# A ConvNeXt-V2 block on one core: from fourteen slots between a block's convolution and its expansion to twelve

## Chip, cores and metric

The kernel runs on one core of a Trainium2 chip. The metric is the device time of one execution in microseconds, as the median over several runs. Before the change it is 1508.79 us (three runs: 1506.65, 1508.79, 1514.91).

## What is computed

The input `x` is an image of 512 x 512 pixels with 96 channels, in bf16. Each pixel gets a depthwise 3 x 3 convolution, a layer norm over its channels, an expansion to 384 channels with a GELU, a global response norm (GRN) over the whole image, a projection back to 96 channels, and the input added:

```python
out = sum over i, j of xp[:, i:i+H, j:j+W, :] * dw[i, j]
h = _layernorm(out, axis=-1)
h = _gelu(jnp.einsum('bhwc,ce->bhwe', h, w1))
gx = jnp.sqrt((h * h).sum(axis=(1, 2), keepdims=True) + 1e-6)
nx = gx / (gx.mean(axis=-1, keepdims=True) + 1e-6)
h = grn_gamma * (h * nx) + grn_beta + h
return x + jnp.einsum('bhwe,ec->bhwc', h, w2)
```

The sum of squares over the whole image parts the work in two phases: nothing can be projected before the last pixel is expanded.

## The kernel before

**Tiling.** A block is 4 image rows, 2048 pixels with 96 channels; there are 128 blocks. In the first phase each block is convolved, normed and expanded, and the sums of squares are kept. A quarter of the expanded values (`gsh`, the first 512 pixels) goes to DRAM, and so does the normed image. In the second phase the other three quarters are expanded again, the projection is made, `x` is added and the result stored. The change lies in the first phase and in the hand-over to the second.

**Slots.** The first phase is a loop over slots `s` (L736). In slot `s` block `s` is convolved (`conv_taps`, L424: 72 small matmuls on TensorE, then one ScalarE instruction moves the result from PSUM to `y_bf`), block `s + 2` is transposed on VectorE (`turn_x`, L403) and block `s + 4` loaded (`load_x`, L180). What else a slot holds is written down ahead of the loop (L697 to L729) with `put(slot, what, block)`: a plan made by hand, with a fixed number of slots between the stages. Every engine gets its instructions in program order, since all engines are wrapped in `InOrder` (L22). This is also why most lines of the profile carry L32, the line of that wrapper; one has to go by tile names.

**From convolution to expansion.** Blocks go through the layer norm in batches of four (after a ramp of 1, 1 and 2 that has a way of its own). Call the first block of a batch f. In the steady state, before the change, the plan is:

| step | engine and tile | slot |
|---|---|---|
| squares of a block b (`stage_sq`, L469) | GpSimd `ysq`; in slots without an expansion ScalarE | b+1 (ScalarE: b) |
| sums over channels (`stage_stats`, L477) | TensorE into `SG` | b+2 |
| moments of the batch (`stage_moments`) | VectorE `mom` | f+5 |
| variance and first guess (`stage_rstd`) | GpSimd, 4 small operations | f+6 |
| two Newton steps (`stage_newton`) | GpSimd, 8 small operations, ending in `rstd` | f+7 |
| transpose of `rstd` (`stage_turn`, L564) | VectorE `rt` | f+7, in the middle |
| to DRAM (`stage_rows`, L570) | SyncE, 2 DMAs `r_dram<-rt` | f+8 |
| back, spread over partitions (`stage_bcast`, L588) | SyncE, 4 DMAs `rbc<-r_dram` | f+9 |
| multiply (`stage_norm`, L596) | GpSimd `yn<-y_bf,rbc` | b+10 |
| to DRAM (`stage_write`, L604) | SyncE, 4 DMAs `yn_dram<-yn` | b+11 |
| back, channels on partitions (`stage_read`, L609) | SyncE, 1 DMA `ynT<-yn_dram`, into a ring of six | b+12 |
| expansion with GELU (`mlp_units`, L626) | TensorE, ScalarE `gsh` and `gm`, VectorE `bst` | b+14 |

The write and the read through DRAM bring the block from 32 groups of rows to one row for each channel. In the expansion ScalarE takes TensorE's results from PSUM through the GELU, VectorE takes statistics of them (`bn_stats`, tile `bst`, and now and then an aggregation, `combine`, L687), and TensorE makes the Gram matrix of the part whose squares VectorE has no time for. 128 blocks with a lag of 14 make 142 slots; the first fourteen without an expansion are conv-only (slots 0 to 4, 7, 10 to 16 and 29, since the ramp and the first batches leave holes), and the last fourteen have an expansion only.

**SyncE's order in a slot.** Nearly all DMAs of the first phase are issued by SyncE, at the head of the loop body, in this order: x load, read, write, bcast, rows, and the store of the `gsh` of the slot before.

**Hand-over.** Three slots before the last the pools of the convolution are closed (L845) and the pools of the second phase opened in their place; in the last but two and last but one slots the first loads of the second phase are issued (`stage_load`, L234), which also says which tile of the ring a resident block's normed image is in.

Of the kernel before, what the change touches and what calls it, by code (L numbers as in the profile page):

```python
# [53 lines left out]
def kernel(  # L54
# [33 lines left out]
    def is_res(q):  # L88
        return q >= NBLK - RES
# [4 lines left out]
    def kept_quads(q):  # L94
        return 2 if is_res(q) else 1
# [16 lines left out]
    def yn_rows(q):  # L112
        k = kept_quads(q) * 128
        return yn_dram[q:q + 2].rearrange("q c (r w) -> (q c) r w", r=GR)[0:128, :, k:]
# [30 lines left out]
    res_g = {q: prepool.tile([128, 2, NCH, QW], bf16, name=f"resg{q}") for q in range(NBLK - RES, NBLK)}  # L145
    NYT = 6
    yn_ring = [prepool.tile([128, GR, W], bf16, name=f"ynT{i}") for i in range(NYT)]

    ynts = {}
# [10 lines left out]
    with ExitStack() as p1:  # L160
# [19 lines left out]
        def load_x(b):  # L180
            t = xinpool.tile([128, SL, C], bf16, name="xin")
            off = x.offset + b * GR * W * C
            rows = lambda p0, p1, s0, s1: (
                t[p0:p1, s0:s1, :].rearrange("p g c -> p (g c)"),
                bass.AP(x.tensor, off + (p0 * PXP - 1 + s0) * C, [[PXP * C, p1 - p0], [1, (s1 - s0) * C]]))
            if b == 0:
                pool.memset(t[0:1, 0, :], 0.0)
                parts = [(16, 128, 0, SL), (0, 16, 1, SL), (1, 16, 0, 1)]
            elif b == NBLK - 1:
                pool.memset(t[96:128, SL - 1, :], 0.0)  # L190
                parts = [(0, 112, 0, SL), (112, 128, 0, SL - 1), (112, 127, SL - 1, SL)]
            else:
                parts = [(0, 128, 0, SL)]
            for part in parts:
                o, i_ = rows(*part)
                sp.dma_start(out=o, in_=i_)
            xins[b] = t
# [36 lines left out]
        def stage_load(n, sq, pq):  # L234
            q = ORDER[n]
            v = (ORDER[0] + n) % NYT
            r0 = q * GR
            if is_res(q):
                kept, ynt = res_g[q], ynts[q]
            else:  # L240
                kept = late.gl.tile([128, 1, NCH, QW], bf16, name="gl")
                (pq if q % 3 == 0 else sq).dma_start(
                    out=kept[:].rearrange("p t j w -> p (t j w)"), in_=g_dram[q])
                ynt = yn_ring[v]
                sq.dma_start(out=ynt[:, :, kept_quads(q) * 128:], in_=yn_rows(q))
            xr = late.xr.tile([128, PXP, C], bf16, name="xr")
            pq.dma_start(out=xr[:], in_=x[0, r0:r0 + GR].rearrange("r w c -> (r w) c").rearrange(  # L247
                "(p g) c -> p g c", g=PXP))
            grp[q] = dict(kept=kept, ynt=ynt, xr=xr)
# [259 lines left out]
        def stage_newton(k, eng):  # L509
            N = BATCHES[k][1] * GR * NG  # L510
            var, rcur = rns[k]
            for it in range(NEWTON_ITERS):
                last = it == NEWTON_ITERS - 1
                t_ = small.tile([128, NS], f32, name="nt")
                eng.tensor_tensor(out=t_[:, :N], in0=rcur, in1=rcur, op=ALU.mult)
                eng.tensor_tensor(out=t_[:, :N], in0=t_[:, :N], in1=var[:, :N], op=ALU.mult)
                eng.tensor_scalar(out=t_[:, :N], in0=t_[:, :N], scalar1=-0.5, scalar2=1.5, op0=ALU.mult, op1=ALU.add)
                rn = small.tile([128, NS], bf16 if last else f32, name="rstd" if last else "rn")
                if last and N % 32:
                    eng.memset(rn[:, N:(N + 31) // 32 * 32], 0.0)  # L520
                eng.tensor_tensor(out=rn[:, :N], in0=t_[:, :N], in1=rcur, op=ALU.mult)
                rcur = rn[:, :N]
            rns[k] = rn
# [46 lines left out]
        def stage_rows(k):  # L570
            b0, n = BATCHES[k]
            rt = rts.pop(k)
            N = n * GR * NG
            nq, nt = min(32, N), (N + 31) // 32
            with nc.allow_non_contiguous_dma("small rows of rstd"):
                if nq == 32:
                    for t in range(nt):
                        sp.dma_start(
                            out=r_dram[b0:b0 + n].rearrange("b r w -> (b r w)").rearrange(
                                "(t q a p) -> t a q p", q=32, a=4, p=32)[t],  # L580
                            in_=rt[:, 32 * t:32 * t + 32])
                else:
                    for a in range(4):
                        sp.dma_start(
                            out=r_dram[b0:b0 + n].rearrange("b r (g m) -> (b r g) m", g=NG)[:, 32 * a:32 * a + 32],
                            in_=rt[32 * a:32 * a + nq, :32])

        def stage_bcast(k):  # L588
            b0, n = BATCHES[k]
            rbc = rbcpool.tile([128, BATCH, W], bf16, name="rbc")  # L590
            for j in range(GR):
                sp.dma_start(out=rbc[32 * j:32 * j + 32, :n, :].rearrange("p n w -> p (n w)"),
                             in_=bass.AP(r_dram[b0].tensor, r_dram[b0].offset + j * n * W, [[0, 32], [1, n * W]]))
            rbcs[k] = rbc
# [9 lines left out]
        def stage_write(b):  # L604
            yn = yns.pop(b)
            for r in range(GR):
                sp.dma_start(out=yn_dst(b, r), in_=yn[32 * r:32 * r + 32, :, :])
# [89 lines left out]
        def put(s, what, v):  # L697
            at.setdefault((s, what), []).append(v)

        RAMP = 4  # L700
        last_norm = -1
        mlp_slots = set()
        for k, (b0, n) in enumerate(BATCHES):
            for b in range(b0, b0 + n):
                quick = b not in mlp_slots
                put(b if quick else b + 1, "sqa" if quick else "sqp", b)
                last_s = b + 1 if quick else b + 2
                put(last_s, "stats", b)
            ramp = b0 + n <= RAMP
            if ramp:  # L710
                put(last_s, "chain", k)
                put(last_s + 1, "spread", k)
            else:
                put(last_s, "moments", k)
                put(last_s + 1, "rstd", k)
                put(last_s + 2, "newton", k)
                put(last_s + 2, "turn", k)
                put(last_s + 3, "rows", k)
                put(last_s + 4, "bcast", k)
            for b in range(b0, b0 + n):  # L720
                last_norm = s = max(last_norm + 1, last_s + (1 if ramp else 5))
                put(s, "norma" if ramp else "norm", b)
                put(s + 1, "write", b)
                put(s + 2, "read", b)
                m = s + (3 if ramp else 4)
                mlp_slots.add(m)
                put(m, "mlp", b)
                put(m, "combine", b)
                put(m + (b < NBLK - 1), "gram", b)  # L729
                last_slot = m  # L730
# [4 lines left out]
        store = None  # L735
        for s in range(last_slot + 1):  # L736
            get = lambda kind: at.get((s, kind), [])
            if s + 4 < NBLK:
                load_x(s + 4)
            for b in get("read"):  # L740
                stage_read(b)
            for b in get("write"):
                stage_write(b)
            for k in get("bcast"):
                stage_bcast(k)
            for k in get("rows"):
                stage_rows(k)
            if store:
                store()
                store = None  # L750
            for k in get("newton"):
                stage_newton(k, pool)
            for b in get("norm"):
# [88 lines left out]
                setup_rest()  # L842
            for b in get("combine"):
                combine(b)
            if s == last_slot - 3:  # L845
                pc.close()
                late.psO = p2.enter_context(tc.tile_pool(name="psO", side="right", bufs=2, space=bass.MemoryType.PSUM))
                late.xr = p2.enter_context(tc.tile_pool(name="xr", side="right", bufs=5))
                late.xb = p2.enter_context(tc.tile_pool(name="xb", side="right", bufs=3))
                late.gr = p2.enter_context(tc.tile_pool(name="gr", side="right", bufs=4))  # L850
                late.gl = p2.enter_context(tc.tile_pool(name="gld", side="right", bufs=6))
                late.o = p2.enter_context(tc.tile_pool(name="o", side="right", bufs=4))
            for n in {2: (0, 1, 2), 1: (3, 4)}.get(last_slot - s, ()):
                stage_load(n, sp, pool)
# [107 lines left out]
```

## Time and profile before

| | |
|---|---|
| median of three runs | 1508.79 us |
| the profiled execution | 1506.65 us, its span 1504.8 us |
| PE (TensorE) busy | 1415.3 us, 94% |
| ACT (ScalarE) busy | 1450.9 us, 96% |
| DVE (VectorE) busy | 1193.5 us, 79% |
| POOL (GpSimd) busy | 1309.6 us, 87% |
| first phase | to about 963 us |
| mean DMA rate | 284 GB/s; 241 to 260 in most of the first phase, 362 to 391 in the second |

The span is what the profiler saw from the first to the last instruction. An engine's share of the whole span mixes three parts with different limits: a head that fills the pipeline, the middle of the first phase, and the second phase. So the text goes by stretches. "Idle before" an instruction is the time its engine waited just before it, with the engine or DMA that ended the wait. SPq is SyncE's queue; its entries are the times that it takes to issue a DMA, not the transfers. In the names of tiles, `U` and `Y` are PSUM banks, `xT` the transposed input, `SG` the sums.

### The profile page before, as it was taken

Reading aid. Unit: us, or ns where it says so; the run is one execution under the profiler, and the core shown is the slowest. Engines: PE = TensorE matmul, PEld = TensorE weight load, DVE = VectorE, ACT = ScalarE, POOL = GpSimd, SP = SyncE. Lnnn points to the kernel's source line nnn. Section 1 sums busy time; section 2 is a strip of 40 time slices with the busy share of each in tenths; the row PEclk is TensorE's granted clock in tenths of the full one; section 3 lists DMA queues with packets and bytes.
Section 4 is the critical chain, followed back from the end, with each engine's and each line's share of the span. In section 5 each row is a group of like instructions: output and inputs, shape, how many; then the busy total and the mean of one; then the engine's idle time right before and its main releaser. Section 6 shows DMA issues by size and latency. Waiting matters only on the chain.

```text
span 1504.8 us, 54858 instructions
## 1 busy us (share of the span) xinstructions
PE 1415.3 (94%) x23110; PEld 815.8 (54%) x23110; DVE 1193.5 (79%) x2149; ACT 1450.9 (96%) x1699; POOL 1309.6 (87%) x934
## 2 busy tenths in 40 slices
PE   8888999999999999999999987799999999999998
PEld 3434444444444444444444443477777777676776
DVE  7759999999999999999999999755555555455555
ACT  7898999999999999999999999899999999899997
POOL 3469899999999999989999987199999999899998
PEclk9999999999999999999999999999999999999999
DMA  6568787888888888888888777799999999999996
GB/s 177 175 199 255 227 257 241 252 260 242 245 256 250 256 260 244 252 252 249 248 265 243 221 216 252 237 340 388 378 391 385 380 378 376 362 367 382 378 378 237
DMA packets 235181, 427.10 MB, mean 284 GB/s; under 512 B 34006, under 2 KB 148278, under 8 KB 234934
## 3 DMA queue, kind: packets, MB, share of 16 engines
q1 hardware_dynamic: 219972, 356.59, 73.7%
q0 software_dynamic: 13600, 66.86, 11.7%
q8 instruction: 181, 2.97, 0.8%
q14 instruction: 66, 0.54, 0.1%
q10 hardware_dynamic: 1362, 0.15, 0.1%
HBM read 272.78 MB, written 150.72 MB: 281 GB/s over the span
## 4 chain that ended last, share of the span: by engine, by line
POOL 22%; PE 20%; ACT 12%; DVE 10%; DMA 8%; issue 3%; SPq 3%; POOLq 0%; ACTq 0%
POOL xb L279 13%; PE U L32 10%; PE O L32 9%; DVE bst L32 7%; ACT gsh L32 6%; ACT gm L32 4%; SPq L32 3%; POOL yn L32 3%; DMA ynT<-yn_dram 2%; DMA yn_dram<-yn 2%; ACT y_bf L32 2%; POOL ysq L32 2%; DMA xin<-in_x_dram 2%; DVE xT L32 2%; POOL xr L247 1%
## 5 line engine op out<-in xcount | busy, mean ns | idle before, releaser
L32 PE MATMUL U<-ynT,w1p 128*128 128x512 bf16 x2292 | 651.7, 381 | 37.3 <-ACT gsh L32 9.6
L32 ACT ACTIVATE gr<-U 128x1536 bf16<-128x1536 f32 (+1 forms) x386 | 519.3, 1449 | 13.5 <-PE U L32 12.8
L32 DVE BATCH_NORM_STATS2 bst<-gsh 128x6 f32<-128x512 bf16 x756 | 465.4, 673 | 20.0 <-ACT gsh L32 19.5
L32 DVE TENSOR_TENSOR o_sb<-O,xb 128x384 bf16<-128x384 f32 x512 | 277.7, 556 | 254.1 <-PE O L32 157.5
L32 POOL TENSOR_TENSOR yn<-y_bf,rbc 128x1536 bf16<-128x1536 bf16 x126 | 391.5, 3109 | 70.7 <-DMA rbc<-r_dram 26.4
L279 POOL TENSOR_TENSOR xb<-xr,B2c 128x1536 f32<-128x1536 bf16 x126 | 394.8, 3135 | 34.0 <-DVE B2c L32 27.2
L32 ACT ACTIVATE gm<-U 128x512 bf16<-128x512 f32 (+1 forms) x640 | 419.8, 803 | 3.9 <-PE U L32 3.8
L32 ACT ACTIVATE gsh<-U 128x1024 bf16<-128x1024 f32 x504 | 375.0, 872 | 5.7 <-PE U L32 4.1
L32 PE MATMUL Y<-xT,Wq 64*32 64x511 bf16 (+1 forms) x8694 | 321.7, 387 | 21.4 <-ACT y_bf L32 9.5
L32 POOL TENSOR_TENSOR ysq<-y_bf 128x1536 bf16<-128x1536 bf16 x114 | 314.1, 2756 | 11.4 <-ACT y_bf L32 11.4
L32 PEld LDWEIGHTS <-w1p 128*128 128x128 bf16 x2292 | 183.1, 98 | 241.3 <-issue 141.5
L32 PEld LDWEIGHTS <-gr 128*128 128x128 bf16 x4584 | 236.8, 98 | 106.3 <-issue 21.2
L32 PE MATMUL O<-W2s,gr 128*128 128x96 bf16 x4584 | 257.2, 206 | 11.5 <-DVE o_sb L32 11.0
L32 DVE BATCH_NORM_STATS2 bst<-gm 128x6 f32<-128x512 bf16 x378 | 232.9, 671 | 0.2 <-ACT gm L32 0.2
L32 PEld LDWEIGHTS <-Wq 64*32 64x32 bf16 x9216 | 113.1, 90 | 199.1 <-issue 150.5
L32 ACT ACTIVATE y_bf<-Y 128x1536 bf16<-128x1536 f32 x121 | 188.0, 1554 | 8.5 <-DMA gam_bf<-in_grn_gamma_dram 4.4
L32 DVE STREAM_TRANSPOSE xT<-xin 128x576 f32<-128x576 f32 (+1 forms) x256 | 181.2, 748 | 0.0
L32 PEld LDWEIGHTS <-gm 128*128 128x128 bf16 x1560 | 99.3, 98 | 84.9 <-issue 52.2
L32 PE MATMUL SG<-gm 128*128 128x128 bf16 x1560 | 130.3, 220 | 1.9 <-DVE SG L32 1.2
L32 PE MATMUL U<-w1p,ynT 128*128 128x384 bf16 (+2 forms) x780 | 127.3, 272 | 1.4 <-ACT resg L32 0.2
L247 POOL DMA_DIRECT2D xr<-in_x_dram x123 | 68.1, 554 | 38.5 <-POOL xb L279 35.6
L32 PE MATMUL O<-W2s,gl 128*128 128x96 bf16 x1512 | 85.4, 207 | 0.0
(105 smaller groups left out, 674.9 us busy)
## 6 DMA issues: line engine op xcount, KB each, us to landing
ynT<-yn_dram SPq DMA_DIRECT2D x254, 384.0 KB
xin<-in_x_dram SPq DMA_DIRECT2D x126, 432.0 KB
yn_dram<-yn SPq DMA_DIRECT2D x512, 96.0 KB
xr<-in_x_dram POOLq DMA_DIRECT2D x128, 384.0 KB, 6.6
out_dram<-o_sb SPq DMA_DIRECT2D x127, 384.0 KB
g_dram<-gsh SPq DMA_DIRECT2D x126, 384.0 KB
gl<-g_dram SPq DMA_DIRECT2D x84, 384.0 KB
gl<-g_dram POOLq DMA_DIRECT2D x42, 384.0 KB, 7.2
```

What stands on the lines that cost most here:

```text
L32: r = f(*a, **k)
L247: pq.dma_start(out=xr[:], in_=x[0, r0:r0 + GR].rearrange("r w c -> (r w) c").rearrange("(p g) c -> p g c", g=PXP))
L279: pq.tensor_tensor(out=xb[:], in0=grp[q]["xr"][:], in1=bias[:, None, :].to_broadcast([128, PXP, C]), op=ALU.add)
```

## The change

Four edits:

1. The plan: `bcast` goes into the slot of `rows` (f+8 in place of f+9), `norm` one slot earlier (b+9), and the expansion three slots after the norm and not four (b+12). Write and read keep their distance to the norm.
2. SyncE's order in a slot: rows, x load, read, write, store, bcast, in place of x load, read, write, bcast, rows, store.
3. The pools of the convolution close two slots before the last, in the same slot as the first loads of the second phase, ahead of them.
4. A resident block's normed image is named by its place in the ring, since its read comes later in the program than its `stage_load`. It is the same tile.

There are then 140 slots; conv-only are 0 to 4, 7, 10 to 14 and 23, and the last twelve have an expansion only. The set-up ahead of the loop is the same in both.

```diff
@@ -236,7 +236,7 @@
             if is_res(q):
-                kept, ynt = res_g[q], ynts[q]
+                kept, ynt = res_g[q], yn_ring[v]
             else:
@@ -716,13 +716,13 @@
                 put(last_s + 2, "newton", k)
                 put(last_s + 2, "turn", k)
                 put(last_s + 3, "rows", k)
-                put(last_s + 4, "bcast", k)
+                put(last_s + 3, "bcast", k)
             for b in range(b0, b0 + n):
-                last_norm = s = max(last_norm + 1, last_s + (1 if ramp else 5))
+                last_norm = s = max(last_norm + 1, last_s + (1 if ramp else 4))
                 put(s, "norma" if ramp else "norm", b)
                 put(s + 1, "write", b)
                 put(s + 2, "read", b)
-                m = s + (3 if ramp else 4)
+                m = s + 3
                 mlp_slots.add(m)
@@ -735,19 +735,19 @@
         for s in range(last_slot + 1):
             get = lambda kind: at.get((s, kind), [])
+            for k in get("rows"):
+                stage_rows(k)
             if s + 4 < NBLK:
                 load_x(s + 4)
             for b in get("read"):
                 stage_read(b)
             for b in get("write"):
                 stage_write(b)
-            for k in get("bcast"):
-                stage_bcast(k)
-            for k in get("rows"):
-                stage_rows(k)
             if store:
                 store()
                 store = None
+            for k in get("bcast"):
+                stage_bcast(k)
             for k in get("newton"):
                 stage_newton(k, pool)
@@ -842,7 +842,7 @@
-            if s == last_slot - 3:
+            if s == last_slot - 2:
                 pc.close()
```

## The prediction

> **What bounds the kernel now.** I read the busy time by stretch first, to see which engine sets the pace where; then the instructions in order of time over three slots in the middle; then ScalarE's idle times; then the landings of the DMAs. A "slot" is one turn of the loop at L736: convolution of block s and, once the pipeline is full, the expansion (`mlp`) of an older block.
>
> Busy time by stretch (columns: stretch and its length, then PE, PEld, DVE, ACT, POOL busy with counts, clock, DMA share, GB/s):
>
> ```profile
> 93.00:190.00 97.00, 86.70 (x1558) 41.25 (x1564) 85.77 (x146) 88.13 (x125) 81.07 (x62) 0.96 0.82 245
> 500.00:700.00 200.00, 192.96 (x3496) 94.50 (x3503) 199.04 (x343) 199.77 (x285) 188.47 (x141) 1.00 0.83 251
> 980.00:1505.00 525.00, 509.67 (x7186) 371.12 (x7184) 274.43 (x507) 505.59 (x373) 477.92 (x285) 1.00 1.00 366
> ```
>
> From 190 to 880 us ScalarE is busy 99.9% and VectorE 99.5%: no schedule shortens that stretch, and any wait put into it is added in full. After 980 us the second phase runs, which the change leaves alone. What can be won lies in the head, where ScalarE waits:
>
> ```profile
> 116.96 0.60 ACT L32 ACTIVATE gm<-U 128x512 bf16<-128x512 f32 x1 [3.02 <-PE U L32]
> 119.57 1.51 ACT L32 ACTIVATE gsh<-U 128x1024 bf16<-128x1024 f32 x2 [2.01 <-PE U L32]
> ```
>
> Two slots of the middle, all engines (start, length, engine, what):
>
> ```profile
> 401.42 2.98 ACT L32 ACTIVATE gsh<-U 128x1024 bf16<-128x1024 f32 x4
> 402.30 0.23 DVE L32 STREAM_TRANSPOSE rt<-rstd 128x64 bf16<-128x64 bf16 x1
> 404.31 1.18 SPq L32 DMA_DIRECT2D r_dram<-rt  x2
> 405.59 0.41 SPq L32 DMA_DIRECT2D g_dram<-gsh  x1
> ...
> 407.48 0.33 SPq L32 DMA_DIRECT2D ynT<-yn_dram  x1
> 407.85 2.56 SPq L32 DMA_DIRECT2D yn_dram<-yn  x4
> 408.47 2.96 ACT L32 ACTIVATE gsh<-U 128x1024 bf16<-128x1024 f32 x4
> 410.44 2.10 SPq L32 DMA_DIRECT2D rbc<-r_dram  x4
> 412.64 0.37 SPq L32 DMA_DIRECT2D g_dram<-gsh  x1
> 413.11 0.38 SPq L32 DMA_DIRECT2D xin<-in_x_dram  x1
> 413.59 1.65 SPq L32 DMA_DIRECT2D ynT<-yn_dram  x1
> ```
>
> The first `gsh` of a slot marks its start: 401.42, 408.47, so 7.04 us a slot, 28.2 a batch of four. SyncE issues in program order. Its `rows` (`r_dram<-rt`) at 404.31 stand behind a write of `yn`; the transpose they need was done at 402.53.
>
> **What the Trainium skill says.** "DMA: Bandwidth & Descriptors", section on the anatomy of one DMA: DMA engines do not wait on semaphores, the issuing sequencer does, before dispatch. So a DMA at the head of SyncE's queue whose data is late holds back all behind it. The trace agrees: SyncE waits 137.7 us in 149 places for `yn_dram<-yn` to land, one of them before 413.59. Same page, "Two DMAs through the same engine are not ordered": a read of what another DMA wrote has to wait for its landing. So write and read-back of a block cost two full trips. Same page, "Issuing engines are not separate DMA queues": all transfers interleave on the same 16 engines; with these at 0.83 here, landings scatter widely. "Perfetto Trace Analysis", section on TensorE instructions: ACT, DVE and GpSimd are strict FIFO. The trace agrees: `rt` runs at 402.30 though its `rstd` was ready at 398.7.
>
> **The change, part by part.** In the terms of a batch with first block f: statistics are complete in slot f+5, `newton` and `turn` stay in slot f+7, `rows` stay in f+8 but go to the head of the slot, `bcast` moves from f+9 to f+8 and behind the store, `norm` of f from f+10 to f+9, its write and read move along, its expansion from f+14 to f+12. Same instructions, same bytes; 140 slots, not 142.
>
> *Head, gains.* Slots with a convolution only fall from 14 to 12. Each of these squares on ScalarE (1.48 us) rather than GpSimd: 2 x 1.48 = 3.0. The two that go (y_bf at 86.65 and 90.10) also had 1.05 and 0.42 of idle: 1.5. The waits at 114 to 121.5 (3.02 + 2.01 + 0.43 = 5.5) come from GpSimd being late: its norm of block 8 stood 8.51 us for the broadcast, so `ysq` of 17 was late for the statistics in TensorE's order. A slot earlier, with the next `rstd` chain (4.5 us) one slot later, I take that as gone.
>
> *Head, loss.* The broadcast of blocks 4 to 7 landed at 77.2, and GpSimd waited for it; it hangs on the transpose at 68.3, which doesn't move. So norm 4 stays at 77.2, its read-back at 85.69, landed at 90.3 (last increment of its semaphore in the trace). The two slots that lay before its expansion are gone: ScalarE reaches it at 86.6 and waits until 90.3 + 1.0 (landing to first `gsh`, as measured on block 0: 29.7 to 30.7): 4.7. Net of the head: 3.0 + 1.5 + 5.5 - 4.7 = 5.3 gained.
>
> *Middle, the new wait.* This decides. Take the third block of the batch before, f-2: normed in slot f+7, written in f+8, read in f+9, expanded in f+10. In SyncE's slot f+8 the order is now rows, x load, read of f-3, write of f-2. The write can't go before the rows, and these not before the turn:
> - turn starts 6.0, 6.9 or 7.9 us after the start of slot f+7, in turns (batches 48, 56, 52: 372.3, 429.5, 402.3 against 366.2, 422.5, 394.4); VectorE falls 1.9 behind when an aggregation comes by and recovers 1 us a batch. Take 6.0;
> - its 0.23 and the semaphore, 0.26; rows 1.22 with the gap after them; x load 0.45; read of f-3 0.36; 0.06: write starts at 8.35;
> - from the first write to the landed read-back: from the trace's landings, over the 23 such blocks between 190 and 880 us, 12.1 to 15.2, median 13.2 (block 50: written from 407.84, landed 413.24, read from 413.58, landed 420.10: 12.3). Between them lie a broadcast, a store and an x load, before and after the change alike. SyncE will have stood idle for some 4 us ahead of it, so the DMA queue is emptier: I take 12.6;
> - landing to `gsh` 1.0.
>
> Sum 8.35 + 12.6 + 1.0 = 21.95, against three slots of 7.04 = 21.1: **0.85 us short**. Before, the same block had four slots and was not behind the rows: it landed 9.2 us ahead of its use on average. With a late turn the wait is 0.85 + 1.9 less what the previous wait let VectorE recover, some 2.5; then the next is 0.85 again. Three batches: 0.85 + 2.5 + 0.85 = 4.2, 1.4 a batch. Batches 16 to 120 are 27: **38 us**. Nothing covers it: ScalarE and TensorE both stand.
>
> *Other paths there.* Read of f-3, behind the same rows: issued at 7.9, 5.05 to land (mean), 1.0: 14.0 against two slots, 14.1: on the edge, inside the same wait. Broadcast: write start 8.35, plus 8.4 to the landing as now, plus 0.55 for the store put before it, plus 0.3: norm f at 17.6; 16.1 us of GpSimd work on, `newton` of the next batch ends at 33.7, that is 4.1 into its slot f+7 (a batch now being 28.2 + 1.4), before VectorE turns it at 6.0: hidden. If that cover goes (a slower landing by 1.9), each us counts. x loads delayed by the rows are used two slots later: nothing. GpSimd's queue keeps the same 12 small operations, now before the third norm of a batch rather than the second: nothing by itself.
>
> *Set-up.* The short title speaks of it; the diff doesn't touch it: 0.
>
> *Tail.* Expansion-only slots fall from 14 to 12, but ScalarE is full in them too (75.0 of 77 us from 880): gain 0. The last two batches have no x load between, slots are 5.7 us, three are 17.1: about even, +1. Pools close in the same slot as the loads that need them, not one before: the loads wait for the last `yn` write either way (xr issued at 929.6, used at 935): 0.
>
> *Sum.* 38 - 5.3 + 1 = +33.7. Profiled execution: 1506.65 (span 1504.8 and 1.85 around it), so 1540.4; the median of the runs shown is 2.1 above it: **1542**.
>
> Bounds of the unknown: with 12.1 for the trip and 0.7 to the `gsh` (TensorE's first matmul of a slot to the first `gsh`: 400.73 to 401.42) the shortage is 0.05, 0.6 to 0.7 a batch with the late turns: 18 us. With 13.2, 1.45, and VectorE not recovering (mean turn 6.9): 2.4 a batch, 65 us. Below nothing the wait itself can't go, since ScalarE is full: the most to be won is the head.
>
> **The rivals.**
> 1. *The trip fits* (not slower). If the emptied queue brings write and read-back to 10 us or so, even turns at 7.9 fit (10.25 + 10 + 1.0 = 21.25), and only the head is left: 1508.8 - 5.3 = 1503.5. For it: a write into an idle queue lands in 2.2, a read-back in 3.8. Against: broadcast, store and x load stay between them. It decides below a trip of about 10.
> 2. *The broadcast alone binds*. GpSimd already stands about 0.6 us a batch for it; the store before it adds 0.55, part of it beyond the cover: 0.4 x 27 = 11, - 5.3: 1514. Against: GpSimd has 6% idle.
> 3. *VectorE never recovers*, or the read of f-3 waits on top: the upper bound, 65 - 5 + 1: 1570.
>
> **How the numbers follow.** Forecast (1520 to 1556) 0.52, rival 1 0.12, rival 2 with the lower bound (1507 to 1520) 0.20, rival 3 0.16. The range 1504 to 1566 leaves out about half of rivals 1 and 3. A measurement of this kernel tells about 0.5% from no change, 7.5 us: faster, below 1501.3, a part of rival 1: 0.06; same, to 1516.3, the rest of it and most of rival 2: 0.20; slower 0.74.
>
> **What would show it.** Right: SyncE waits for `rt` in most batches ahead of `r_dram<-rt`, some 3 to 4 us; ScalarE's `gsh` waits on TensorE once a batch, at the third block, by 1 to 2.5 us; ScalarE's share from 190 to 880 falls from 99.9% to about 95%; slots 15 on begin at about 91 us; the wait near 117 is gone. Wrong: ScalarE still at 99.9% in the middle (rival 1), or GpSimd full and waiting for `rbc` each batch with SyncE not waiting for `rt` (rival 2). A trip that differs by 1 us from 12.6 moves the time by about 25 us: that is the number I am least sure of.

## The result, and the profile after

The changed kernel takes **1558.32 us** (median of four runs, 1555.51 to 1565.27), the kernel before 1507.72 in the same job (four runs). The ratio is 1.0333, with a 95% interval from 1.0285 to 1.038: slower. The profiled execution took 1559.01 us, its span 1557.1; before it was 1506.65 and 1504.8. So 52.3 us of span have to be found.

Where they came in is read from ScalarE's first `gsh` (or `resg`) of a block, in both traces:

| first GELU of block | before | after | difference |
|---|---|---|---|
| 3 | 59.1 | 62.9 | +3.8 |
| 18 | 203.8 | 203.1 | -0.7 |
| 116 | 892.7 | 930.5 | +37.8 |
| 125 | 944.9 | 985.6 | +40.7 |
| 126 | 950.4 | 1001.5 | +51.1 |
| end of the span | 1504.8 | 1557.1 | +52.3 |

From block 18 to 116 the loss is 38.5 us, block 126 alone adds 10.4, and the head wins 4.5 after a slip of 3.8. The slip came before block 3, where SyncE's queue has the same order in both; in the experiments, all with the same start, block 3 comes at 58.5 to 61.8, so I take it for this execution's and not for the change's. (TensorE's granted clock was 0.50 of full speed from 30.4 to 40.7 us in this execution, and 1.00 in the one of the kernel before.) From block 19 to 107, over 22 batches, a batch takes 29.64 us in place of 28.20. This **period** is used below to compare kernels.

The busy time by stretch of the kernel after (stretch, length, then PE, PEld, DVE, ACT, POOL, clock, DMA share, GB/s):

```profile
93.00:190.00 97.00, 88.90 (x1574) 41.68 (x1573) 87.59 (x148) 90.25 (x127) 78.25 (x60) 0.97 0.76 229
500.00:700.00 200.00, 185.65 (x3358) 91.17 (x3357) 191.18 (x326) 193.38 (x276) 182.11 (x139) 1.00 0.78 239
```

In the middle every engine lost busy time together, ScalarE from 199.77 to 193.38 of 200 us: so each of them now waits, and none of the five sets the pace by its own work. Which waits those are is read on SyncE's queue and on TensorE. SyncE before, then after:

```profile
SPq L32 <- DVE bst L32: 9.9, 21, 1.0
```

```profile
SPq L32 <- DVE bst L32: 122.3, 32, 7.2
```

TensorE after:

```profile
PE U L32 <- DMA ynT<-yn_dram: 54.6, 32, 10.4
```

(Total, times, longest.) SyncE waits for VectorE 32 times. The releaser named is `bst`, the instruction next to the turn in VectorE's queue; the timeline shows that it is the turn: 28 of the 32 end with the issue of the rows, 4.3 us on average. TensorE waits for a read-back 32 times; before once, 1.3 us. One batch of the kernel after (f = 80; slot f+7 starts at 622.8), first SyncE's queue:

```profile
625.14 0.59 SPq L32 DMA_DIRECT2D g_dram<-gsh  x1
631.26 1.17 SPq L32 DMA_DIRECT2D r_dram<-rt  x2
632.48 0.47 SPq L32 DMA_DIRECT2D xin<-in_x_dram  x1
633.12 0.33 SPq L32 DMA_DIRECT2D ynT<-yn_dram  x1
633.50 2.73 SPq L32 DMA_DIRECT2D yn_dram<-yn  x4
636.33 0.54 SPq L32 DMA_DIRECT2D g_dram<-gsh  x1
636.91 1.88 SPq L32 DMA_DIRECT2D rbc<-r_dram  x4
638.83 0.42 SPq L32 DMA_DIRECT2D xin<-in_x_dram  x1
639.36 0.37 SPq L32 DMA_DIRECT2D ynT<-yn_dram  x1
```

VectorE, in the same stretch:

```profile
628.66 2.43 DVE L32 BATCH_NORM_STATS2 bst<-gsh 128x6 f32<-128x512 bf16 x4
631.01 0.23 DVE L32 STREAM_TRANSPOSE rt<-rstd 128x64 bf16<-128x64 bf16 x1
```

And ScalarE:

```profile
629.77 2.99 ACT L32 ACTIVATE gsh<-U 128x1024 bf16<-128x1024 f32 x4
...
638.16 2.92 ACT L32 ACTIVATE gsh<-U 128x1024 bf16<-128x1024 f32 x4 [1.19 <-issue]
...
646.75 2.92 ACT L32 ACTIVATE gsh<-U 128x1024 bf16<-128x1024 f32 x4 [1.45 <-issue]
```

SyncE is done with its slot at 625.73 and then stands until the turn, which starts at 631.01, has run. Then all goes out at once: rows, x load, the read of block 77 (f-3) at 633.12, the write of 78 (f-2) at 633.50. Block 77's read-back lands at 637.4 and ScalarE starts on it at 638.16, 1.19 us late; block 78's write lands, its read is issued at 639.36 and lands at 646.0, and ScalarE starts at 646.75, another 1.45 us late. The two slots begin 8.39 and 8.59 us after the ones before, in place of 7.04. (A landing is the last increment of the DMA's semaphore in the trace.)

Over all blocks from 19 to 116 ScalarE stands 29.1 us ahead of the first `gsh` of a slot; in the kernel before it was 0.9. 17.2 us of it are at the third block of a batch (18 batches of 24), 11.9 at the second (11 of 24), none at the others.

A long wait costs more than its own length. Each of the five longest of these, 1.61 to 3.15 us, runs into a stretch of 3.4 or 6.8 us in which TensorE's granted clock is 0.50 (491.2 to 494.6, for one), and in each the second `gsh` waits another 0.70 to 0.82 us for TensorE, 3.9 us in all. The next longest, 1.45 us, does not. Over all runs every such wait of more than 2.2 us ran into half the clock, and none of less than 1.0. The clock is not what makes the waits: of the 97 slots from block 19 to 115, 87 have no half clock, and these have 19.8 us of the 37.4 us by which the 97 are longer than 7.04 each.

In the head a wait at block 4 has come and the one near 117 us is gone; at the end of the first phase there is one long wait, at block 126:

```profile
94.82 1.51 ACT L32 ACTIVATE gsh<-U 128x1024 bf16<-128x1024 f32 x2 [4.42 <-PE U L32]
97.20 0.60 ACT L32 ACTIVATE gsh<-U 128x512 bf16<-128x512 f32 x1 [0.87 <-PE U L32]
...
117.20 2.98 ACT L32 ACTIVATE gsh<-U 128x1024 bf16<-128x1024 f32 x4
119.97 1.18 ACT L32 ACTIVATE gm<-U 128x512 bf16<-128x512 f32 x2
```

```profile
1001.53 3.14 ACT L32 ACTIVATE resg<-U 128x1024 bf16<-128x1024 f32 x4 [10.02 <-PE U L32]
```

### The profile page after: what moved, and what is told of

Read it like the earlier page. It is cut to its first block, busy times and chain, and to the rows that moved or that the text cites. A ratio compares the mean times of both kernels' runs of the same rounds, so it can differ in the third digit from the quotient of the medians.

```text
span 1557.1 us, 54806 instructions
## 1 busy us (share of the span) xinstructions
PE 1426.9 (92%) x23110; PEld 818.8 (53%) x23110; DVE 1199.2 (77%) x2149; ACT 1453.8 (93%) x1696; POOL 1315.2 (84%) x936
## 4 chain that ended last, share of the span: by engine, by line
POOL 18%; PE 18%; ACT 6%; DMA 4%; issue 3%; DVE 2%; SPq 1%; POOLq 0%; ACTq 0%
POOL xb L279 14%; PE U L32 9%; PE O L32 8%; ACT gsh L32 3%; DMA ynT<-yn_dram 2%; ACT gm L32 2%; POOL xr L247 2%; POOL gl L242 1%; DVE o_sb L32 1%; ACT y_bf L32 1%; SPq L32 1%; DMA yn_dram<-yn 1%; POOL yn L32 1%; PE Y L32 1%; DVE bst L32 1%
## 5 line engine op out<-in xcount | busy, mean ns | idle before, releaser
L32 PE MATMUL U<-ynT,w1p 128*128 128x512 bf16 x2292 | 659.7, 386 | 83.3 <-DMA ynT<-yn_dram 54.6
L32 ACT ACTIVATE gr<-U 128x1536 bf16<-128x1536 f32 (+1 forms) x386 | 520.1, 1448 | 13.4 <-PE U L32 12.6
L32 DVE BATCH_NORM_STATS2 bst<-gsh 128x6 f32<-128x512 bf16 x756 | 466.4, 673 | 51.4 <-ACT gsh L32 50.6
L32 ACT ACTIVATE gsh<-U 128x1024 bf16<-128x1024 f32 x504 | 374.2, 855 | 47.2 <-issue 21.5
L32 PE MATMUL Y<-xT,Wq 64*32 64x511 bf16 (+1 forms) x8766 | 327.1, 391 | 18.6 <-ACT y_bf L32 6.0
L32 POOL TENSOR_TENSOR ysq<-y_bf 128x1536 bf16<-128x1536 bf16 x116 | 318.7, 2748 | 12.3 <-ACT y_bf L32 12.3
L32 PE MATMUL O<-W2s,gr 128*128 128x96 bf16 x4584 | 256.6, 206 | 13.0 <-DVE o_sb L32 12.6
L247 POOL DMA_DIRECT2D xr<-in_x_dram x123 | 68.1, 554 | 38.5 <-POOL xb L279 35.3
```

Source lines behind the costliest of these rows:

```text
L32: r = f(*a, **k)
```

## The experiments

In the expectations **theory A** is the forecast's: the rows at the head of SyncE's slot wait for the turn, the writes and reads behind them are late, and with three slots from norm to expansion the read-back is late too. e1, e2 and e3 name a rival B of their own, that the loop through GpSimd and the broadcast sets the pace; in e6 and e9 **B** is: three slots are too few wherever the rows stand; and **C**, from e8 on, is: the norm a slot sooner tightens the way through GpSimd and the broadcast, and the late read-backs only follow. All runs, with the time's ratio to the kernel before in the same job (whose median was 1506.13 to 1508.24 us in the four jobs), the period of a batch, and ScalarE's idle time ahead of the first `gsh` of blocks 19 to 116. "Slots" is the distance from norm to expansion:

| kernel | norm | slots | rows | median us | ratio (95%) | period | first-`gsh` waits |
|---|---|---|---|---|---|---|---|
| before | f+10 | 4 | late in the slot | 1507.72 | 1 | 28.20 | 0.9 |
| after | f+9 | 3 | head | 1558.32 | 1.0333 (1.0285 to 1.038) | 29.64 | 29.1 |
| e1_lag13 | f+9 | 4 | head | 1537.12 | 1.0208 (1.018 to 1.0235) | 29.27 | 15.3 |
| e2_turn_late | f+9 | 3 | head | 1602.85 | 1.0645 (1.0614 to 1.0676) | 31.53 | 58.2 |
| e3_turn_early | f+9 | 3 | head | 1538.83 | 1.0218 (1.0191 to 1.0244) | 29.25 | 21.5 |
| e4_tail | f+9 | 3 | head | 1556.33 | 1.0336 (1.0287 to 1.0385) | 29.40 | 24.9 |
| e5_tail_late | f+9 | 3 | head | 1548.59 | 1.0264 (1.0224 to 1.0303) | 29.77 | 30.8 |
| e6_three_slots | f+10 | 3 | late in the slot | 1510.66 | 1.002 (1.0009 to 1.003) | 28.16 | 0.1 |
| e7_rows_head | f+10 | 4 | head | 1501.63 | 0.9962 (0.9947 to 0.9977) | 28.18 | 0.6 |
| e8_three_and_rows | f+10 | 3 | head | 1553.80 | 1.0314 (1.0293 to 1.0335) | 29.78 | 29.0 |
| e9_rows_back | f+9 | 3 | behind the write | 1538.68 | 1.0203 (1.0179 to 1.0227) | 29.27 | 18.5 |
| e11_three_rows_mid | f+10 | 3 | behind the write | 1514.00 | 1.0049 (1.0033 to 1.0064) | 28.52 | 6.2 |
| e12_rows_turn_late | f+10 | 4 | head | 1503.40 | 0.9973 (0.9963 to 0.9983) | 28.18 | 0.7 |
| e13_lag13_rows_back | f+9 | 4 | behind the write | 1536.12 | 1.0199 (1.017 to 1.0228) | 29.25 | 16.2 |

All edits below are against the changed kernel. In e6, e8, e11 and e13 block 28 also takes its squares a slot later, on GpSimd, so that its sums stay with its own batch.

### The slot given back: e1_lag13

```diff
-                m = s + 3
+                m = s + (3 if ramp else 4)
```

> The changed kernel with the expansion four slots behind the norm again (lag 13), SyncE's order and the earlier broadcast kept. Theory A (a block's write and read-back stand behind rows that wait for the turn, and three slots are too short for that): the first gsh of a slot no longer waits, because the read-back has 7 us more; the 34 us of waits of ScalarE between blocks 19 and 116 fall under 3 us, and a batch takes 28.2 us again. Theory B (GpSimd's loop through the broadcast sets the pace): a batch stays near 29.6 us, since nothing in that loop is changed. Time by A: 1558 less 34, and less up to 10 if the late read of block 126 is hidden too: 1512 to 1525. By B: 1555.

It took 1537.12, which neither theory had. This kernel leaves out the late squares of block 28: its sums are added to those of block 24 and cleared with that batch, so the norms of blocks 24 and 28 come out wrong. The instructions are the same but for that one squaring, which ScalarE does, and e13, which keeps the sums of block 28 apart, has the same period. The read-backs now land 6.3 to 9.4 us ahead of their use on average, so the wait of theory A is gone, though ScalarE's first `gsh` still waits 15.3 us and not under 3, now mostly at the first block of a batch. And the period is 29.27, not 28.2: something else stands close behind. What waits is another pair. TensorE waits for `ysq`:

```profile
PE SG L32 <- POOL ysq L32: 32.1, 25, 5.2
```

(before: 4.1, once), and GpSimd, which makes it, had waited for the broadcast:

```profile
POOL yn L32 <- DMA rbc<-r_dram: 38.7, 16, 7.6
POOL yn L32 <- DMA xin<-in_x_dram: 33.6, 10, 9.5
```

(The second line is the same wait: `yn` needs no `xin`; the norm at 487.22, for one, starts 0.07 us after the last of the four broadcasts issued from 480.56 on has landed.) Theory A alone doesn't give this number, and theory C was formed here.

### The size of the disputed delay: e2_turn_late and e3_turn_early

e2 puts the turn behind `squares_rest`, 1.9 us later on VectorE; e3 ahead of `squares(2)`, 1.24 us earlier:

```diff
-                for k in get("turn"):
-                    stage_turn(k)
                 conv(2)
...
                 squares_rest()
+                for k in get("turn"):
+                    stage_turn(k)
```

> The changed kernel with the transpose of rstd moved 1.9 us later in VectorE's order, behind the three statistics of the slot. Theory A: each batch whose third or second block already waits waits 1.9 us longer, less what VectorE recovers: between 1.2 and 1.9 in 24 to 27 batches, 30 to 50 us, 1590 to 1608. Theory B (the loop of GpSimd and the broadcast, with the rows hidden under the norm): under 10 us more.

> The changed kernel with the transpose of rstd two statistics (1.24 us) earlier in VectorE's order. Theory A: up to 1.2 us a batch less, less where rstd comes later than the turn: 12 to 25 us, 1533 to 1546. Theory B: no change to speak of, within 5 us. A third possibility is that VectorE now stands waiting for rstd and loses what is won.

Both fell into A's range. Later by 1.9, the period grew by 1.89, one for one, and the waits moved to the second block (42.1 us in 23 of 24 batches). Earlier by 1.24 in VectorE's order, it shrank by only 0.39, to 29.25. In e3's trace the turn follows the end of `newton` within 0.3 us in 13 of 25 batches (7 in the kernel after): there it can't come earlier, since `rstd` isn't there. So the turn is on the path that sets the period, and there is a floor under it at 29.25, which e1 met too.

### Part by part: e6_three_slots, e7_rows_head, e8_three_and_rows

e6 is the kernel before with the three slots alone, e7 the kernel before with the rows at the head and the earlier broadcast alone, e8 has both; the norm stays at f+10 in all three.

```diff
 e8, and with the m of e1 also e7
-                last_norm = s = max(last_norm + 1, last_s + (1 if ramp else 4))
+                last_norm = s = max(last_norm + 1, last_s + (1 if ramp else 5))
 e6, besides: the queue's old order (bcast, rows, store behind the write) and
-                put(last_s + 3, "bcast", k)
+                put(last_s + 4, "bcast", k)
```

> The kernel before with one part of the change alone: the expansion three slots after the norm, not four (lag 13). Norm at f+10, broadcast at f+9 and SyncE's old order (rows last but for the store) stay. Theory A (the wait is made by rows at the head of the queue together with three slots): the third block's write starts 0.6 us ahead of its slot and not 1 to 4 us into it, its read-back lands about 2 us ahead of its use: few waits, batch 28.2 to 28.4 us, 1500 to 1513. Theory B (three slots are too few for write and read-back wherever the rows stand): waits of the first gsh once a batch, 1530 or more.

> The kernel before with the other part alone: rows at the head of the slot, broadcast a slot sooner and behind the store; norm at f+10 and the expansion four slots after it stay (lag 14). SyncE will wait for the turn as in the changed kernel, and the third block's write will be as late, but it has a slot more. Theory A: nothing waits for it, 1503 to 1512, GpSimd's waits for the broadcast gone. If the rows at the head cost something by themselves (stores or x loads held back), 1520 or more.

> Both parts that cost nothing each on its own, together: rows at the head of the slot with the broadcast a slot sooner (lag 14 with that: 1501.6) and the expansion three slots after the norm (lag 13 with that: 1510.7); norm stays at f+10, so that the loop of GpSimd and the broadcast has room. The block written behind the rows is now f-3. In the lag-14 run it was written 8.5 to 10.4 us after the start of slot f+7 and its read-back landed at 20.5 to 23.0; three slots give it until 21.1 less 0.7. Theory A (the read-back behind the rows binds, as forecast): first gsh waits once a batch at b%4 = 1 and sometimes the block before, 25 to 35 us in all, 1530 to 1550. Theory C (the norm a slot sooner, thus the broadcast loop, was the true limit, and the late read-backs only its follower): 1502 to 1515.

The middle of e6 (ScalarE full) and of e7 (full as well), and of e8:

```profile
500.00:700.00 200.00, 192.63 (x3508) 94.58 (x3504) 199.29 (x343) 200.00 (x285) 191.73 (x143) 1.00 0.84 256
```

```profile
500.00:700.00 200.00, 192.82 (x3500) 94.94 (x3499) 199.15 (x342) 199.79 (x285) 188.62 (x146) 1.00 0.82 254
```

```profile
500.00:700.00 200.00, 184.99 (x3329) 90.59 (x3321) 189.68 (x325) 191.14 (x271) 179.75 (x128) 0.98 0.79 239
```

Each part alone costs the middle nothing (e6 lost 3.3 us in all, and at its block 126, on which more below, ScalarE waits 5.4); together they cost 46 us (1553.8 against 1508.2). B falls by e6. C falls as the whole cause by e8: there `newton` ends on average 0.5 us *before* slot f+7 begins, 7 us ahead of the turn, so GpSimd is off the path, and the period is 29.78 all the same. What binds is A: the block behind the rows is now f-3. In e8 it is written 8.5 to 10.8 us after the start of slot f+7, its read-back lands at 20.3 to 23.7 (batches 44 to 116), and it is due at 21.1: a wait of that block or the one before it in 20 of 24 batches. In e7 it is written 8.5 to 10.4 and lands at 20.5 to 23.0 (batches 52 to 92), the very same, but due at 28.1. The wait for the turn in e7's queue, batch 80 (slot f+7 from 587.9):

```profile
592.19 0.59 SPq L32 DMA_DIRECT2D g_dram<-gsh  x1
594.21 1.19 SPq L32 DMA_DIRECT2D r_dram<-rt  x2
595.45 0.47 SPq L32 DMA_DIRECT2D xin<-in_x_dram  x1
596.10 0.33 SPq L32 DMA_DIRECT2D ynT<-yn_dram  x1
596.48 2.55 SPq L32 DMA_DIRECT2D yn_dram<-yn  x4
```

The distances between these issues are those of the kernel after, and the wait ahead of them is harmless here.

e7 is also faster than before, by 0.4%, and the lowest of all here, though e12 is not told apart from it. The gain is the head's: GpSimd waits 3.63 us and not 8.51 for the broadcast of batch 8, and ScalarE's waits of 5.5 us near 117 are gone. ScalarE's idle time up to its first instruction of the second phase is 26.8 us against 32.1.

### Is the covered delay really covered? e12_rows_turn_late

e7 with the late turn of e2.

> The lag-14 kernel with rows at the head (1501.6) and the turn 1.9 us later on VectorE, the same edit that made the changed kernel 44 us slower (1602.9 against 1558.3). Theory A: the read-backs land 6 us or more ahead of their use there, so the delay is covered: 1500 to 1506. If the turn's delay acts by another way than the read-backs of three slots: over 1520.

1503.40, period 28.18, and SyncE's wait is there in the profile:

```profile
SPq L32 <- DVE rt L32: 72.8, 26, 9.1
```

The same edit that cost 44.5 us in the kernel after costs nothing here that these runs can tell (1501.63 against 1503.40; the intervals of their ratios overlap). The read-back of f-3 still lands 4.4 us ahead of its use on average.

### The floor: e9_rows_back and e13_lag13_rows_back

Rows and broadcast go behind the write and ahead of the store, so that no write stands behind the turn; e13 also has the four slots of e1.

```diff
-            for k in get("rows"):
-                stage_rows(k)
             if s + 4 < NBLK:
                 load_x(s + 4)
...
             for b in get("write"):
                 stage_write(b)
+            for k in get("rows"):
+                stage_rows(k)
+            for k in get("bcast"):
+                stage_bcast(k)
             if store:
```

> The changed kernel (lag 12, norm at f+9) with rows and then the broadcast right behind the write, ahead of the store: x load, read, write, rows, broadcast, store. The write of the third block no longer stands behind the turn, and the broadcast is issued at about 12 us after the start of slot f+7 and not 14. Theory A: waits of the first gsh fall from 29 us to below 10, and the loop of GpSimd and broadcast gets 2 us of room: 1508 to 1525. Theory B (three slots are too few anyhow): 1540 or more. The wait of block 126 at the end of the phase (10 us) stays in it either way.

> The lag-13 kernel with norm at f+9 and the expansion four slots after it, now with rows and broadcast behind the write and ahead of the store. The lag-13 run with rows at the head took 1537 with no read-back late. Theory C (norm at f+9 leaves only two norms between the write that the broadcast stands behind, f-2's, and the norm that needs it: a loop of 19 us of GpSimd's work and some 10 us from the end of norm f-2 to the landed broadcast, 29 us a batch): still 1525 to 1540, GpSimd waits for rbc in nearly every batch. If instead it was the wait for the turn at the head of the queue: 1500 to 1512.

e9 missed A's range: 1538.7, period 29.27, and 18.5 us of first-`gsh` waits where A had under 10. e13 came out as C has it: 29.25. With e1 and e3 these are four kernels with two orders of SyncE's queue, three and four slots, one period, and one thing in common: norm at f+9. All kernels with norm at f+10 that keep their read-backs in time (e6, e7, e12) have 28.2. The closest pair is e1 and e7, whose plans differ in nothing but the slot of the norm, with all that follows it (and in block 28): 29.27 against 28.18. In e13 GpSimd waits for the broadcast 24 times:

```profile
POOL yn L32 <- DMA rbc<-r_dram: 64.2, 24, 10.8
```

The loop can be followed in the traces, here in e1 for the batch f = 60:

```profile
471.66 0.32 POOL L32 TENSOR_TENSOR rstd<-nt,rn 128x64 bf16<-128x64 f32 x1
475.06 1.16 SPq L32 DMA_DIRECT2D r_dram<-rt  x2
480.56 2.43 SPq L32 DMA_DIRECT2D rbc<-r_dram  x4
487.22 3.10 POOL L32 TENSOR_TENSOR yn<-y_bf,rbc 128x1536 bf16<-128x1536 bf16 x1 [3.68 <-DMA xin<-in_x_dram]
```

With norm at f+9, the end of the next batch's `newton` comes 16.1 us after the start of norm f (16.0 to 16.1 on average in each of after, e1, e3, e9, e13: GpSimd's own work, without a gap). From the end of `newton` to the start of the next batch's norm f it is 13.1 to 13.4 us in e1, e3, e9 and e13: turn, rows, write, broadcast and its landing. The two make up the period, 29.2 to 29.5. With norm at f+10 the first stretch is 10.3 us, since `newton` then stands ahead of norm f-3 in GpSimd's queue and not ahead of norm f-2: one norm and one squaring more cover the chain.

In e9 the late read-back of f-2 (18.2 us of waits) is a follower: its write starts 0.29 us after its norm ends, so GpSimd is late, not the queue.

### The end of the phase: e4_tail and e5_tail_late

There are two suspects for the 10.02 us at block 126. GpSimd's queue and SyncE's in the kernel after:

```profile
978.95 1.28 POOL L32 DMA_DIRECT2D xr<-in_x_dram  x2
980.22 0.54 POOL L32 DMA_DIRECT2D gl<-g_dram  x1
980.75 1.59 POOL L32 DMA_DIRECT2D xr<-in_x_dram  x3
```

```profile
980.15 2.92 SPq L32 DMA_DIRECT2D yn_dram<-yn  x4
983.12 0.59 SPq L32 DMA_DIRECT2D g_dram<-gsh  x1
990.07 0.58 SPq L245 DMA_DIRECT2D ynT<-yn_dram  x1
990.83 0.48 SPq L32 DMA_DIRECT2D ynT<-yn_dram  x1
```

A load of the second phase (L245) is issued by SyncE at 990.07, ahead of the block's read at 990.83; e4 keeps it behind. And from 978.95 on GpSimd's queue issues five loads of x and one of g, around the block's write at 980.15; e5 lets SyncE issue them behind the last read-backs (with e4's edit):

```diff
-            for n in {2: (0, 1, 2), 1: (3, 4)}.get(last_slot - s, ()):
-                stage_load(n, sp, pool)
+            for n in {1: (0, 1, 2), 0: (3, 4)}.get(last_slot - s, ()):
+                stage_load(n, sp, sp)
...
-                stage_load(n + PRE, nc.sync, nc.gpsimd)
+                stage_load(n + PRE, sp, nc.gpsimd)
```

> The changed kernel with the loads of the second phase issued in program order too, so that the first of them no longer stands ahead of the read of block 126 in SyncE's queue. If that order is the cause of the 10 us that ScalarE stands before block 126: these go, 1558 less 8 to 11 = 1547 to 1550, and nothing else changes in the first phase. If the read is late for another reason (a slow landing beside the other loads): the wait stays, 1558.

> The changed kernel with the first loads of the second phase issued by SyncE, a slot later each, behind the last read-backs (before: x by GpSimd's queue as soon as its last norm is done). In the changed kernel the write of block 126 took some 8 us to be seen, beside five loads of x and one of g from GpSimd's queue, and its expansion then stood 10.0 us. If that burst is what slows write and read-back of block 126, the wait falls below 2 us and the time to 1547 to 1552; if the wait stays near 9, the burst is not the cause: 1555 to 1560. If the second phase now starts late for want of x, 1560 or more.

From block 126 to its first instruction of the second phase ScalarE waits 12.0 us in the kernel after, 9.1 in e4, with the same time, and 1.0 in e5. (That last 1.0 is the step to the second phase, and every kernel has it.) The ratio falls from 1.0333 to 1.0264; the intervals of the two overlap, so it is the trace that shows the gain. In e5's trace block 126 runs without a wait:

```profile
991.95 3.16 ACT L32 ACTIVATE gm<-U 128x512 bf16<-128x512 f32 x5
994.82 3.11 ACT L32 ACTIVATE resg<-U 128x1024 bf16<-128x1024 f32 x4
```

So the loads from the other queue were most of it: from its first issue to its last landing the write takes 10.6 us in the kernel after, 10.9 in e4 and 4.5 in e5. It was 10.4 in the kernel before as well; four slots hid that. In the kernel after the read-back behind it took 9.6 us too (990.83 to 1000.41), beside three more loads from GpSimd's queue and SyncE's at 990.07; in e4 7.4, in e5 3.4.

### A version that might beat all: e11_three_rows_mid

Lag 13, norm at f+10, rows and broadcast behind the write, e5's tail.

> A version that might beat both: lag 13, norm at f+10, expansion three slots after it, rows and at once the broadcast (a slot sooner than before, at f+8) behind the write and ahead of the store, and the first loads of the second phase by SyncE behind the last read-backs. By theory A no write stands behind the turn; by C the broadcast isn't behind the write of f-2; the tail's wait of 6 us in the lag-13 run (1510.7) goes: 1498 to 1506. If read-backs behind the rows' wait are late, waits of the first gsh and 1510 or more.

It took 1514.0, and missed. The tail's wait is gone (block 126 doesn't wait), but the second block of a batch waits in 11 of 24 batches, 6.1 us in all: its read is issued 2.8 us after its write has landed, since the broadcast, which has to wait for the rows to land, stands ahead of it in SyncE's queue. e7 and e12 stay the best.

## Why the prediction was right, and which steps were not

Predicted were 1542 in a range from 1504 to 1566, and slower with 0.74; it is 1558, slower. That is in the range, but 2 us above the band of the forecast proper (1520 to 1556), in the part given to rival 3: the change cost 50.6 us in place of 33.7. The range held; the sum of the parts was too small, mostly behind block 116.

- **The new wait in the middle: right in kind, and close in size.** 38 us were forecast for the 27 batches from 16 to 120; from block 18 to 116, 24.5 batches, it is 38.5, and to block 125 41.4. The terms, measured on f-2 in the kernel after: write to landed read-back 12.3 us on average (5.66 to land, 0.83 to the read, 5.80 to land), against 12.6; write start 8.4 to 10.8, against 8.35 and the late turns; landing to `gsh` 0.74 in most places where ScalarE waits, against 1.0. Between the first `gsh` of block 19 and that of 116 ScalarE waits 33.8 us with the smaller ones (1.7 before), 1.4 a batch, as forecast. The rest of the 38.5 is its busy time there, 686.5 us against 680.1: its instructions overlap by 175.4 us in place of 192.4. e8 shows the mechanism without any other, e2 its slope, e7 and e12 that a fourth slot covers it.
- **"Read of f-3 ... on the edge, inside the same wait": wrong.** That sum was made with the even turn, 6.0. After a late turn f-3's read is issued at 10.3 and it waits itself (11.9 us of the 29.1); f-2 behind it then waits for its own part. So the total held by some luck: the late turns had been counted at f-2 alone. That f-3 would wait on top is what rival 3 had.
- **"Broadcast: ... hidden": wrong, though it didn't show in the time.** The forecast had norm f at 17.6, 16.1 us of GpSimd's work to the next `newton`, and so `newton` 1.9 us ahead of the turn. The 16.1 is what is measured. Norm f starts at 18.8 on average, and in e1 at 19.7: of the chain from `newton`, the turn waits 0.9 us for its place in VectorE's queue (e1), and from rows to broadcast it takes 6.1 us (e1) where the terms of the forecast (1.22 + 0.45 + 0.36 + 0.06, the write's 2.6, the store's 0.55) give 5.24. And the sentence that `newton`'s new place in GpSimd's queue costs "nothing by itself" left out that it took 5.8 us of cover from this chain. The true price of the loop alone is 29.25 - 28.2 = 1.05 us a batch, not rival 2's 0.4.
- **Why that didn't show in the time.** The two limits act on the same batches, and the larger decides: 29.64 from the read-backs over 29.25 from the loop. Summed they would have been 1.44 + 1.05. Taking the read-backs away (e1) wins only 0.37 a batch, taking the loop away (e8) nothing.
- **The head: right.** 5.3 forecast, 4.5 won from block 3 to block 18: the wait at 117 is gone, and block 4 waits 4.42 + 0.87 = 5.3 us, against 4.7. One thing was left out: the first of the old waits near 117 ran into half the clock (0.50 from 114.0 to 120.8), so the 2.01 + 0.43 behind it need not be GpSimd's lateness alone; the new wait did too (91.9 to 98.7).
- **The tail: wrong, 10 us.** "Pools close in the same slot ... 0" looked at when the loads could start and not at what they would do to the write of block 126 beside them. Its write took 10.6 us to land, where the middle has 5.7, and its read-back 9.6, where the middle has 5.8; "three are 17.1: about even" had no room for that.
- **The sum.** Forecast +33.7: -5.3, +38, +1. Measured +52.3: +3.8 slip, -4.5, +38.5, and from block 116 on +14.5, of which block 126 has 10.4. Of the signs that were named, all came: SyncE's wait for the turn, 4.3 us, ScalarE's waits at the third block (0.2 to 2.1 us, and at the second 0.3 to 3.2), its share at 193.4 of 200 (95% forecast, 96.7% found; from 190 to 880 us 656.3 of 690 = 95.1%), the slots from 15 on (94.8, less the slip of 3.8: 91.0), the wait at 117.

That the turn's wait, not some slowing of DMAs, makes the loss in the middle is shown by e2, e7 and e8. That the four kernels at the floor agree to 0.02 us (29.25 to 29.27) though two of them have the rows at the head and two behind the write is partly chance: the chain has other members in each. Of the 4 us of other losses behind block 116, 2.9 come before block 125 and 1.2 after the start of block 126; these runs don't settle more.

Two readings of the forecast were off without weight. VectorE's share from 190 to 880 us is 684.7 of 690 = 99.2%, not 99.5%. And the 2.2 us of a write into an idle queue, in rival 1, is the time from the issue of the last of its four DMAs; from the first issue no write of the kernel before landed in under 4.1 us.

## What to carry to other kernels

A lag between two stages covers the whole chain between them, not only its DMAs: before a slot is taken out, close every loop that runs through it (here two: write and read-back, and `newton` to broadcast), with the waits that stand ahead in each engine's queue. Two edits that are each free can be dear together, when both live on the same slack; and a limit that experiments show alone may be hidden under a larger one. Put a DMA that waits for a late producer where little stands behind it, or leave what stands behind it a slot of room.

## What the runs showed of the hardware

- Six loads issued from GpSimd's queue slowed a write from SyncE's: 384 KB that were issued from 980.15 on, in the midst of them, had landed at 990.71; with those loads issued later (e5), it took from 983.47 to 987.99. In the steady state such a write takes 5.2 to 6.6 us on average, by its place in the batch. That agrees with the Trainium skill ("DMA: Bandwidth & Descriptors", section "Issuing engines are not separate DMA queues"): DMAs of different issuing engines run on the same 16 DMA engines and interleave.
- When TensorE and ScalarE stood long in the middle of the first phase, TensorE's granted clock fell to 0.50 for 3.4 us or more: in blocks 19 to 116 of the kernel after at all five waits of ScalarE's first `gsh` of 1.61 us or more and at none of 1.45 or less; over all runs at every one above 2.2 us, at none below 1.0, and at some between.
- The name of a releaser in the profile can be that of a neighbour: the turn's wait is called `bst` in the kernel after (122.3 us) and `rt` in e12 (72.8), and the wait for the broadcast `rbc` or `xin`. In both cases the timeline of the waiting queue beside that of the producer told which it was.
